# Scores and first mix in an attention kernel as products of 64 rows by 64 columns, in common visits

## The chip, the cores and the metric

The kernel runs on one core of a Trainium2 chip. The metric is device microseconds of one execution; three timed runs of the kernel before have a median of 1301.0 us (1297.99 to 1308.34). The engines are named as in the profile: PE is TensorE (PEld its weight loads), DVE VectorE, ACT ScalarE, POOL GpSimd, SP SyncE.

## The reference

Attention whose heads are mixed before and after the softmax, then two gated feed-forward stages over all tokens. Everything is float32.

```python
# q, k, v: (4, 12, 448, 64); w_pre, w_post: (12, 12)
scores = scale * np.matmul(q, k.transpose(0, 1, 3, 2))
scores = np.einsum('bhij,hg->bgij', scores, w_pre)
scores = scores - np.max(scores, axis=-1, keepdims=True)
attn = np.exp(scores)
attn = attn / (np.sum(attn, axis=-1, keepdims=True) + 1e-09)
attn = np.einsum('bhij,hg->bgij', attn, w_post)
x = np.matmul(attn, v)                     # -> (1792, 768)
x = ((x @ w1) * (x @ w2) @ w3) @ w_out     # first stage, 768 -> 1024 -> 1024 -> 768
h = np.maximum(np.maximum(x @ m1, x @ m2), x @ m3)
return h @ m_out                           # second stage, 768 -> 768 -> 768
```

## The kernel before

**Scores.** A score unit is `scores(b, pr, it)`: 112 queries of one pair of heads. q and k lie with the 64 values of a head on 64 partitions, two heads on 128. So a unit is two products, one on partitions 0 to 63 and one on 64 to 127, each with 112 columns of weights (the queries) and 448 moving columns (the keys), into the two banks of the PSUM tile `s`. Both are plain float32 products; such a product is two matmul rows in the trace. ACT scales and evicts the unit, and it is stored to `sdram` in DRAM, `[query, head, key]`. A batch has 6 x 4 = 24 units, 96 in all.

**First mix and softmax.** `regroup` loads 20 queries back as two blocks of 10, with (query, head) on 120 partitions, one DMA on SP. `mix_softmax` mixes the heads: for each of the two blocks one product with the 120x120 block-diagonal matrix `kp`, into a bank of the tile `m`. The first 62 steps are plain (`plain`): float32, two matmul rows for each product. The other 30 are split: DVE cuts `x` into a high and a low part in `split_scores` (L232, L233), and each product is three fp32r passes (in `products`, L115). DVE then takes the maximum (L250), ACT the exponentials with their sums (L254), and DVE makes `kwr`, the block-diagonal second mixing matrix with the reciprocals of the sums in it (L258 to L261).

**Second mix and v.** `post_mix` (L277) multiplies `e` by `kwr` for the step before, into `p`; ACT evicts it to `a`. After six steps (120 queries) `attend` (L304) multiplies by v, head by head, two heads on the two halves of the columns.

**The dense stages.** Batches 0 and 1 are finished under the attention as fillers: generators that yield after six fp32r passes (w in the rows: `products`, L115). Batches 2 and 3 come after the attention, in `last_two`. Weights arrive as 64-bit words and are cut by ACT and DVE the first time (`from_f64`), later loaded back from DRAM by SP (`slab`, L157 to L159).

**Order.** The main loop has a step for each 20 queries, 23 for a batch, 92 in all. A step calls `regroup` two steps ahead, `split_scores` one step ahead, `mix_softmax`, and then three thirds, in which fillers run at 2.7 or 3.9 yields a step, the units of the next batch are placed (`ahead_scores`), and `post_mix` and `attend` come. What one engine is given stays in program order on it; a tile scheduler moves work by its own priorities before that. The tile `m` exists once (two banks), `s` once, `p` once.

Of the kernel before, what the change touches and what calls it, by code (L numbers as in the profile page):

```python
# [7 lines left out]
F32 = mybir.dt.float32  # L8
# [9 lines left out]
P = 128  # L18
GI = 10
NG = -(-S // GI)  # L20
CG = 12
JC, JP = 4, 112
IT = 4
# [8 lines left out]
PLAIN = 2 * NP + 16  # L32
# [18 lines left out]
def plain(b, p):  # L51

    return b * NP + p < PLAIN
# [3 lines left out]
def attention_talking_heads_moe_kernel(  # L57
# [106 lines left out]
    kp = const.tile([120, GI, H], F32, name="kp")  # L164
    kp_hi = const.tile([120, GI * H], F32R, name="kp_hi")
    kp_lo = const.tile([120, GI * H], F32R, name="kp_lo")
    kw = const.tile([120, H, GI], F32, name="kw")

    def block_diagonals():
        own = const.tile([120, GI], F32, name="own")  # L170
        wide = const.tile([120, 2, H], F32, name="wide")
        nc.gpsimd.dma_start(own, block_mask)
        for x, w in enumerate((w_pre, w_post)):
            nc.gpsimd.dma_start(wide[:, x], bass.AP(w.tensor, w.offset, [[0, GI], [H, H], [1, H]]))
        nc.vector.tensor_mul(
            kp, wide[:, 0].unsqueeze(1).to_broadcast([120, GI, H]), own.unsqueeze(2).to_broadcast([120, GI, H])
        )
        nc.vector.tensor_mul(
            kw, wide[:, 1].unsqueeze(2).to_broadcast([120, H, GI]), own.unsqueeze(1).to_broadcast([120, H, GI])
        )  # L180
        flat = kp.rearrange("p i h -> p (i h)")
        nc.vector.tensor_copy(kp_hi, flat)
        nc.vector.tensor_sub(kp_lo, flat, kp_hi.bitcast(F32))
# [3 lines left out]
    def load_heads():  # L187

        t = [big.tile([P, HP, S], F32, tag=x, name=n) for x, n in (("xhi", "kall"), ("xlo", "qall"))]
        for a, z in ((0, 2), (2, HP)):  # L190
            for dst, src, w in zip(t, (kT, qT), (S, JP)):
                nc.sync.dma_start(dst[:, a:z, :w], src[0, a:z, :, :w].rearrange("x p j -> p x j"))
        nc.sync.dma_start(t[1][:, :, JP:], qT[0, :, :, JP:].rearrange("x p j -> p x j"))
# [8 lines left out]
    def scores(b, pr, it, heads, tag="s", eng=None, out=None):  # L202
        k, q = heads
        st = out if out is not None else pa.tile([JP, 2, S], F32, tag="s", name="s", bufs=2)
        pt = banks(tag)
        for o in range(2):
            sl = slice(o * D, (o + 1) * D)
            nc.tensor.matmul(pt[:JP, o, :S], q[sl, it * JP:(it + 1) * JP], k[sl], start=True, stop=True)  # L208
        if eng is nc.vector:
            nc.vector.tensor_scalar_mul(st, pt[:JP, :, :S], D ** -0.5)  # L210
        else:
            nc.scalar.activation(st, pt[:JP, :, :S], AF.Copy, scale=D ** -0.5)  # L212
        if out is None:
            issue = nc.sync if eng is nc.vector else nc.scalar
            issue.dma_start(sdram[b][it * JP:(it + 1) * JP, 2 * pr:2 * pr + 2], st)

    def regroup(b, p):
        n, m = groups(p)
        r = m * H
        x = pa.tile([120, 2, S], F32 if plain(b, p) else F32R, tag="x", name="x", bufs=AHEAD + 1)  # L220
        src = sdram[b][2 * GI * p:2 * GI * p + n * m].rearrange("(x i) h j -> (i h) x j", x=n)
        nc.sync.dma_start(x[:r, :n] if plain(b, p) else x[:r, :n].bitcast(F32), src)
        xst[b, p] = x

    def split_scores(b, p):
        if plain(b, p):
            return
        n, m = groups(p)
        r = m * H
        x = xst[b, p]  # L230
        xh = pa.tile([120, 2, S], F32R, tag="xh", name="xh", bufs=2)
        nc.vector.tensor_copy(xh[:r, :n], x[:r, :n].bitcast(F32))  # L232
        nc.vector.tensor_sub(x[:r, :n], x[:r, :n].bitcast(F32), xh[:r, :n].bitcast(F32))  # L233
        xst[b, p] = (x, xh)

    def mix_softmax(b, p):
        n, m = groups(p)
        r = m * H
        pt = banks("m")
        x = xst.pop((b, p))  # L240
        for u in range(n):
            if plain(b, p):
# [6 lines left out]
        nmax = pa.tile([120, 2], F32, tag="nmax", name="nmax", bufs=3)  # L249
        nc.vector.tensor_reduce(out=nmax[:r, :n], in_=pt[:r, :n, :S], axis=AX.X, op=ALU.max, negate=True)  # L250
        e = pa.tile([120, 2, S], F32, tag="e", name="e", bufs=LAG + 1)
        den = pa.tile([120, 2], F32, tag="den", name="den", bufs=3)
# [4 lines left out]
        rec = pa.tile([120, 2], F32, tag="rec", name="rec", bufs=3)  # L257
        nc.vector.tensor_scalar_add(den[:r, :n], den[:r, :n], 1e-9)  # L258
        nc.vector.reciprocal(rec[:r, :n], den[:r, :n])
        kwr = pa.tile([120, 2, H * GI], F32, tag="kwr", name="kwr", bufs=LAG + 1)  # L260
# [6 lines left out]
    def post_mix(b, p):  # L267
        n, m = groups(p)
        r = m * H
# [433 lines left out]
    row = pa.tile([JP, H, S], F32, tag="a", name="row", bufs=1)  # L703
    for pr in range(HP):
        scores(0, pr, 0, first[pr], "mps"[pr % 3], nc.vector if pr % 2 else nc.scalar, row[:, 2 * pr:2 * pr + 2])
        if pr % 2:
            sl = slice(2 * pr - 2, 2 * pr + 2)
            nc.sync.dma_start(sdram[0][:JP, sl], row[:, sl])
# [5 lines left out]
    early = [(pr, it) for it in range(1, IT) for pr in range(HP)]  # L714
    heads = {}

    def ahead_scores(b, p, third):

        if b + 1 < B:
# [114 lines left out]
```

## Time and profile before

| | |
|---|---|
| timed runs | 1297.99, 1301.0, 1308.34 us; median 1301.0 |
| profiled execution: span | 1297.0 us, an execution of its own beside the timed ones; median less span 4.0 us |
| mean granted TensorE clock | 0.976 of full speed |
| busy over the span | PE 1229.3 us (95%), PEld 1009.0, DVE 807.5, ACT 611.0, POOL 222.0 |
| first mix: maximum on DVE | 92 times, from 51.3 to 915.7 us |
| score units | 15.3 to 697.6 us |
| HBM | 176.50 MB read, 84.15 MB written |

PE's busy time is modelled at its ends: matmuls are pipelined, and one of 448 columns shows 0.36 us although the next starts 0.205 us later. What a piece of work costs on PE is therefore read from the starts of what stands around it. The span falls into the start (to about 110 us), attention with score units of the next batch and fillers (to about 700), attention of the last batch with fillers (to about 945), and the dense stages of batches 2 and 3.

### The profile page before, as it was taken

The numbers are of one execution on the slowest core, as the hardware profiler recorded it, in microseconds if no ns is written. First come the engines' busy times: TensorE is split into PE (matmuls) and PEld (weight loads), VectorE is DVE, ScalarE is ACT, GpSimd is POOL, SyncE is SP. The second block draws the span as 40 slices with busy tenths as digits, with TensorE's granted clock in tenths as the row PEclk, the third lists the DMA queues.
The fourth block names the chain that finished last, engine by engine and source line by source line (L and its number), as shares of the span: only waits on it lengthen the run. The fifth ranks groups of instructions, "written<-read, shape, count | busy, mean of one in ns | idle before, by whom it ended". The sixth has DMA issues, their size and how long they took to land.

```text
span 1297.0 us, 19342 instructions
## 1 busy us (share of the span) xinstructions
PE 1229.3 (95%) x7438; PEld 1009.0 (78%) x7438; DVE 807.5 (62%) x1251; ACT 611.0 (47%) x1146; POOL 222.0 (17%) x243
## 2 busy tenths in 40 slices
PE   4588999989999999999998999999989999999998
PEld 1246777867777787777777988999978889989887
DVE  5677334448573466867366686965357766368784
ACT  3466555546564455756454444444353334323331
POOL 3343111000000000000456546650000000000000
PEclk6799999999999999999998999999989999999999
DMA  9978768688786569887787987772353332133334
GB/s 288 297 248 255 211 209 293 181 244 265 246 280 200 166 194 289 287 258 243 241 301 235 274 263 238 247 240 88 123 190 98 108 113 68 45 106 104 110 98 133
DMA packets 111987, 261.92 MB, mean 202 GB/s; under 512 B 22868, under 2 KB 66152, under 8 KB 111896
## 3 DMA queue, kind: packets, MB, share of 16 engines
q1 hardware_dynamic: 55736, 116.71, 30.6%
q0 software_dynamic: 15392, 77.62, 18.1%
q10 hardware_dynamic: 40768, 66.37, 15.2%
q8 instruction: 59, 0.97, 0.3%
q14 instruction: 32, 0.26, 0.1%
HBM read 176.50 MB, written 84.15 MB: 201 GB/s over the span
## 4 chain that ended last, share of the span: by engine, by line
PE 77%; DMA 11%; DVE 8%; ACT 3%; issue 2%; POOL 0%; DVEq 0%; ACTq 0%; SPq 0%; POOLq 0%
PE w L115 34%; PE p L277 9%; PE m L115 8%; PE m L243 6%; PE p L115 6%; PE s L115 5%; PE s L304 5%; PE s L208 4%; DMA xdram<-x 2%; DMA xlo<-xdram 2%; DVE wc L104 2%; DMA wlo<-kept_b 1%; DVE nmax L250 1%; DMA sdram<-s 1%; DMA x<-sdram 1%
## 5 line engine op out<-in xcount | busy, mean ns | idle before, releaser
L254 ACT ACTIVATE e<-m,nmax 120x448 f32<-120x448 f32 x180 | 112.6, 631 | 149.3 <-DVE nmax L250 144.5
L277 PEld LDWEIGHTS p<-kwr,e 120*112 120x112 f32 (+1 forms) x1440 | 162.6, 179 | 18.7 <-issue 6.9
L277 PE MATMUL p<-kwr,e 120*112 120x120 f32 (+1 forms) x1440 | 167.9, 270 | 2.5 <-DVE kwr L261 1.3
L250 DVE TENSOR_REDUCE nmax<-m 120x2 f32<-120x896 f32 (+1 forms) x92 | 98.0, 1065 | 106.6 <-PE m L243 84.9
L159 DVE TENSOR_TENSOR wlo<-wlo,whi 128x768 fp32r<-128x768 f32 (+1 forms) x58 | 67.9, 1171 | 100.6 <-ACT whi L158 96.3
L284 ACT COPY a<-p 112x480 f32<-112x480 f32 (+1 forms) x184 | 92.3, 552 | 59.7 <-PE p L277 54.5
L115 PE MATMUL w<-yhi,whi 128*128 128x448 f32 (+1 forms) x292 | 117.6, 403 | 0.0
L115 PE MATMUL w<-hhi,whi 128*128 128x448 f32 (+1 forms) x280 | 112.3, 401 | 4.6 <-ACT hhi L336 4.0
L243 PE MATMUL m<-x,kp 120*120 120x448 f32 (+1 forms) x244 | 106.5, 556 | 6.3 <-DMA x<-sdram 4.4
L115 PE MATMUL w<-hhi,wlo 128*128 128x448 f32 (+1 forms) x280 | 102.6, 367 | 4.3 <-DVE wlo L159 4.3
L115 PE MATMUL w<-yhi,wlo 128*128 128x448 f32 (+1 forms) x292 | 105.4, 361 | 0.0
L115 PE MATMUL w<-ylo,whi 128*128 128x448 f32 (+1 forms) x292 | 105.2, 360 | 0.0
L115 PE MATMUL w<-hlo,whi 128*128 128x448 f32 (+1 forms) x280 | 102.9, 368 | 0.9 <-POOL hlo L337 0.9
L158 ACT CAST whi<-wlo 128x768 fp32r<-128x768 f32 (+1 forms) x58 | 52.2, 900 | 91.3 <-DMA wlo<-kept_w 22.8
L212 ACT ACTIVATE s<-s 112x896 f32<-112x896 f32 x84 | 77.0, 917 | 19.7 <-PE s L208 13.8
L115 PE MATMUL w<-xhi,whi 128*128 128x448 f32 x192 | 80.1, 417 | 3.7 <-ACT xhi L324 3.7
L208 PE MATMUL s<-k,q 64*112 64x448 f32 x288 | 73.5, 588 | 7.6 <-ACT s L212 3.9
L304 PEld LDWEIGHTS s<-a,v 112*64 112x64 f32 x1536 | 73.7, 137 | 6.2 <-issue 3.7
L304 PE MATMUL s<-a,v 112*64 112x120 f32 (+1 forms) x1536 | 77.1, 260 | 0.7 <-ACT s L212 0.5
L101 ACT ACTIVATE wc<-wraw 128x768 f32<-128x768 f32 (+1 forms) x64 | 54.4, 853 | 46.5 <-DMA wraw<-in_w3T 15.1
L243 PEld LDWEIGHTS m<-x,kp 120*120 120x120 f32 (+1 forms) x244 | 43.6, 185 | 39.8 <-issue 26.8
L115 PEld LDWEIGHTS w<-hhi,whi 128*128 128x128 f32 x280 | 53.6, 191 | 25.7 <-issue 13.3
(205 smaller groups left out, 2615.7 us busy)
## 6 DMA issues: line engine op xcount, KB each, us to landing
x<-sdram SPq DMA_DIRECT2D x88, 420.0 KB, 5.0
sdram<-s ACTq DMA_DIRECT2D x84, 392.0 KB, 4.5
wraw<-in_wm POOLq DMA_DIRECT2D x18, 768.0 KB, 6.7
wlo<-kept_m SPq DMA_DIRECT2D x27, 384.0 KB, 3.0
wlo<-kept_w SPq DMA_DIRECT2D x18, 512.0 KB, 4.4
wraw<-in_w3T POOLq DMA_DIRECT2D x16, 512.0 KB, 6.2
kept_m<-wc ACTq DMA_DIRECT2D x18, 384.0 KB, 4.7
wc<-kept_m POOLq DMA_DIRECT2D x18, 384.0 KB, 6.9
```

Source lines behind the costliest of these rows:

```text
L101: nc.scalar.activation(t, high.bitcast(F32), AF.Abs)
L115: nc.tensor.matmul(out, w, r, start=(k == 0), stop=(k == 3 * n_k - 1))
L158: nc.scalar.copy(hi, t)
L159: nc.vector.tensor_sub(lo, t, hi.bitcast(F32))
L208: nc.tensor.matmul(pt[:JP, o, :S], q[sl, it * JP:(it + 1) * JP], k[sl], start=True, stop=True)
L212: nc.scalar.activation(st, pt[:JP, :, :S], AF.Copy, scale=D ** -0.5)
L243: nc.tensor.matmul(pt[:r, u, :S], kp.rearrange("p i h -> p (i h)")[:r, :r], x[:r, u], start=True, stop=True)
L250: nc.vector.tensor_reduce(out=nmax[:r, :n], in_=pt[:r, :n, :S], axis=AX.X, op=ALU.max, negate=True)
L254: nc.scalar.activation(e[:r, u], pt[:r, u, :S], AF.Exp, bias=nmax[:r, u:u + 1], scale=1.0, accum_out=den[:r, u:u + 1])
L277: nc.tensor.matmul(pt[:, jc // 2, jc % 2, :, u * GI:u * GI + m], e[:r, u, jc * JP:(jc + 1) * JP], kwr[:r, u].rearrange("p (g i) -> p g i", ...
L284: nc.scalar.copy(ast[b][:, 2 * x:2 * x + 2, :, off:off + w].rearrange("p c g i -> p (c g) i"), pt[:, x, :, :, :w].rearrange("p c g i -> p ...
L304: nc.tensor.matmul(pt[o * D:(o + 1) * D, pr // 3, pr % 3, :], vst[b][:, jc, h * D:(h + 1) * D], a[:, jc, h, :], start=(jc == 0), stop=(jc ...
```

## The change

A score unit now is four products, each of 64 rows (the values of a head) by 64 columns (64 queries): two heads of a pair and two halves of 128 queries, each on a quarter of TensorE's array. Since 448 is 3 x 128 + 64, the last 64 queries of two pairs make a unit together (a mixed unit, with two stores). A batch has 21 units, 84 in all. The first batch's first row of units is 128 queries wide.

The mix's blocks hold 5 queries: 60 partitions, with zero columns up to 64. A step still has 20 queries, in four blocks: two on partitions 0 to 59 and two on 64 to 123, and each block's product writes 64 partitions of the tile `m`. `kp` is a matrix of 60 rows by 64 columns, twice, one below the other. `regroup` is two DMAs of 60 partitions. All mixes are plain; `plain`, `split_scores`, `kp_hi` and `kp_lo` are gone. Softmax and second mix run on 128 partitions, with zero rows in `kw`.

A unit is issued right ahead of the mix of its step (`some_scores(0)`), others in the thirds. Units for the next batch go into a list (`waiting`) by a new table of steps, and the pair loads have three buffers and are asked for two steps ahead.

```diff
+GB = GI // 2
+HB = 64
+MR = GB * 12
-PLAIN = 2 * NP + 16
...
+def units():
+
+    for pr in range(0, HP, 2):
+        for x in (pr, pr + 1):
+            for it in range(S // P):
+                yield [(x, P * it), (x, P * it + HB)]
+        yield [(pr, S // P * P), (pr + 1, S // P * P)]
...
+            for r in range(2):
+                nc.gpsimd.dma_start(
+                    wide[HB * r:HB * r + MR, x], bass.AP(w.tensor, w.offset, [[0, GB], [H, H], [1, H]])
+                )
...
-        t = [pa.tile([P, S], F32, tag=x, name=x, bufs=2) for x in "kq"]
+        t = [pa.tile([P, S], F32, tag=x, name=x, bufs=3) for x in "kq"]
...
-        for o in range(2):
-            sl = slice(o * D, (o + 1) * D)
-            nc.tensor.matmul(pt[:JP, o, :S], q[sl, it * JP:(it + 1) * JP], k[sl], start=True, stop=True)
+        for c, (pr, i) in enumerate(unit):
+            k, q = heads[pr]
+            for o in range(2):
+                sl = slice(o * D, (o + 1) * D)
+                nc.tensor.matmul(pt[HB * c:HB * c + HB, o, :S], q[sl, i:i + HB], k[sl], start=True, stop=True)
...
+            (pr, i), (other, _) = unit
+            if other == pr:
+                issue.dma_start(sdram[b][i:i + P, 2 * pr:2 * pr + 2], st)
+            else:
+                for c, (pr, i) in enumerate(unit):
+                    issue.dma_start(sdram[b][i:i + HB, 2 * pr:2 * pr + 2], st[HB * c:HB * c + HB])
+
+    def blocks_of(p):
+
+        i = 2 * GI * p
+        return [[(i + GI * r + GB * c, max(0, min(GB, S - i - GI * r - GB * c))) for c in range(2)] for r in range(2)]
 
     def regroup(b, p):
...
+        x = pa.tile([P, 2, S], F32, tag="x", name="x", bufs=AHEAD + 1)
+        for r, row in enumerate(blocks_of(p)):
+            if row[1][1] == GB:
+                src = sdram[b][row[0][0]:row[0][0] + GI].rearrange("(c i) h j -> (i h) c j", c=2)
+                nc.sync.dma_start(x[HB * r:HB * r + MR], src)
+                continue
...
-    def split_scores(b, p):
...
     def mix_softmax(b, p):
...
-        for u in range(n):
-            if plain(b, p):
-                nc.tensor.matmul(
-                    pt[:r, u, :S], kp.rearrange("p i h -> p (i h)")[:r, :r], x[:r, u], start=True, stop=True
-                )
-            else:
-                for _ in products(pt[:r, u, :S], [(kp_hi[:r, :r], kp_lo[:r, :r], x[1][:r, u], x[0][:r, u])], 1):
-                    pass
...
+        for c in range(2):
+            for u, row in enumerate(blocks_of(p)[:n]):
+                sl = slice(HB * u, HB * u + row[c][1] * H)
+                nc.tensor.matmul(pt[HB * c:HB * c + HB, u, :S], kp[sl], x[sl, c], start=True, stop=True)
...
+    def some_scores(third):
         if early:
...
+            scores(0, early.pop(0), first, "s", nc.vector if third == 1 else nc.scalar)
+        elif waiting:
+            scores(*waiting.pop(0))
...
-            if s + 1 < len(steps):
-                split_scores(*steps[s + 1])
+            ahead_scores(*steps[s])
+            some_scores(0)
             mix_softmax(*steps[s])
...
-            if s < len(steps):
-                ahead_scores(*steps[s], third)
+            if third:
+                some_scores(third)
```

On PE, in the second batch's part of the loop, where the next batch's units are made under the first batch's dense stage, the order before has mix (L243) and unit (L208) apart. In these rows w is a filler's PSUM tile, with its row split (xhi, xlo) and weights (whi, wlo), and x2 counts products:

```order
L115 MATMUL w<-xlo,whi 128x448
L115 MATMUL w<-xhi,wlo 128x448
L243 MATMUL m<-x,kp 120x448 x2
L115 MATMUL w<-xhi,whi 128x448
L115 MATMUL w<-xlo,whi 128x448
L115 MATMUL w<-xhi,wlo 128x448
L115 MATMUL w<-xhi,whi 128x448
L115 MATMUL w<-xlo,whi 128x448
L115 MATMUL w<-xhi,wlo 128x448
L208 MATMUL s<-k,q 112x448 x2
L115 MATMUL w<-xhi,whi 128x448
```

On PE at the like place of the changed program (L121 is the line of the dense products, L216 the units, L256 the mix):

```order
L121 MATMUL w<-xhi,whi 128x448
L121 MATMUL w<-xlo,whi 128x448
L121 MATMUL w<-xhi,wlo 128x448
L216 MATMUL s<-k,q 64x448 x4
L256 MATMUL m<-x,kp 64x448 x4
L121 MATMUL w<-xhi,whi 128x448
L121 MATMUL w<-xlo,whi 128x448
```

The unit has moved up to stand right ahead of the mix, and each of them is four products now. From the seventh mix to the 67th there are 50 such common visits, 10 of a unit alone, 10 of a mix alone and one of two units and a mix; before, 21 visits of that stretch join a unit and a mix, 52 are a unit alone and 41 a mix alone (one of these is half a mix). The last 25 mixes stand alone in both.

On DVE, in the last batch, the order before has the split between the weight slab and the sums (L159 makes the low part of a slab, L412 that of a row of y):

```order
L250 TENSOR_REDUCE nmax<-m 120x2
L159 TENSOR_TENSOR wlo<-wlo,whi 128x1024
L232 CAST xh<-x 120x896
L258 TENSOR_SCALAR den<-den 120x2
L233 TENSOR_TENSOR x<-x,xh 120x896
L259 RECIPROCAL rec<-den 120x2
L261 TENSOR_TENSOR kwr<-kw,rec 120x240
```

On DVE in the changed program:

```order
L258 TENSOR_REDUCE nmax<-m 128x2
L165 TENSOR_TENSOR wlo<-wlo,whi 128x1024
L266 TENSOR_SCALAR den<-den 128x2
L267 RECIPROCAL rec<-den 128x2
L269 TENSOR_TENSOR kwr<-kw,rec 128x240
```

The two instructions of the split are gone; the rest stands in the same order.

On SP, late in the loop, before (L222 is `regroup`, L157 a weight slab loaded back):

```order
L222 DMA x<-sdram_78 120x2x448
L157 DMA wlo<-kept_w_1_84 128x1024
L222 DMA x<-sdram_78 120x2x448
L157 DMA wlo<-kept_w_1_84 128x1024
L222 DMA x<-sdram_78 120x2x448
L157 DMA wlo<-kept_m_0_101 128x768
```

On SP in the changed program, close behind that place:

```order
L163 DMA wlo<-kept_m_0_101 128x768
L240 DMA x<-sdram_78 60x2x448 x2
L163 DMA wlo<-kept_m_0_102 128x768
L240 DMA x<-sdram_78 60x2x448 x2
L163 DMA wlo<-kept_m_0_103 128x768
```

Each regroup is two issues instead of one, in the same turn with the slabs.

## Rows read from the trace of the kernel before

**Rows 1.** The page's slices: PE's busy share in tenths, 40 equal slices.
```profile
PE   4588999989999999999998999999989999999998
```

**Rows 2.** Windows: busy us (x instructions) of each engine, PEclk, DMA share, GB/s.
```profile
0.00:110.00 110.00, 71.89 (x278) 36.73 (x278) 74.82 (x105) 52.40 (x96) 40.38 (x50) 0.83 0.89 276
110.00:700.00 590.00, 577.80 (x3808) 447.27 (x3809) 332.59 (x549) 324.99 (x624) 78.44 (x99) 0.99 0.76 241
700.00:945.00 245.00, 237.94 (x1716) 219.15 (x1714) 160.55 (x218) 107.47 (x227) 103.14 (x95) 0.99 0.69 216
```

**Rows 3.** Waits of PE, 110 to 700 us: who <- whom: us, times, longest.
```profile
PE s L208 <- ACT s L212: 3.9, 5, 1.3
PE w L115 <- ACT xhi L324: 3.7, 1, 3.7
```

**Rows 4.** Timeline of PE, 300 to 330 us: start us, us, engine, line.
```profile
303.31 0.37 PE L115 MATMUL w<-xhi,wlo 128*128 128x448 f32 x1
303.52 1.67 PE L243 MATMUL m<-x,kp 120*120 120x448 f32 x4
...
305.23 0.37 PE L115 MATMUL w<-xlo,whi 128*128 128x448 f32 x1
...
306.05 0.36 PE L115 MATMUL w<-xhi,wlo 128*128 128x448 f32 x1
306.33 1.01 PE L208 MATMUL s<-k,q 64*112 64x448 f32 x4
...
307.58 0.36 PE L115 MATMUL w<-xlo,whi 128*128 128x448 f32 x1
```

**Rows 5.** Timeline of PE cut to starts before 306.6 us: that unit.
```profile
306.33 0.63 PE L208 MATMUL s<-k,q 64*112 64x448 f32 x2
```

**Rows 6.** The product with v: starts to 325.9 us, and its line in all.
```profile
325.82 0.32 PE L304 MATMUL s<-a,v 112*64 112x120 f32 x2
...
L304 PE MATMUL s<-a,v x96: 266/266/317, 325.8 to 330.7; 112*64 112x120 f32 x96
```

**Rows 7.** Timeline of PE at a split mix, 821 us.
```profile
820.65 0.36 PE L115 MATMUL m<-x,kp_hi 120*120 120x448 f32 x1
820.86 0.37 PE L115 MATMUL m<-xh,kp_lo 120*120 120x448 f32 x1
```

**Rows 8.** Groups by line: busy us, mean ns, idle before and releasers: the split.
```profile
L233 DVE TENSOR_TENSOR x<-x,xh 120x896 fp32r<-120x896 f32 (+1 forms) x30 | 35.8, 1193 | 0.7
...
L232 DVE CAST xh<-x 120x896 fp32r<-120x896 f32 (+1 forms) x30 | 24.2, 805 | 6.6 <-DMA x<-sdram 6.6
```

**Rows 9.** Tiles m and s: duration ns min/median/max, first and last start.
```profile
L250 DVE TENSOR_REDUCE nmax<-m x92: 609/1083/1093, 51.3 to 915.7; 120x2 f32<-120x896 f32 x88, 96x1 f32<-96x448 f32 x4
...
L212 ACT ACTIVATE s<-s x84: 897/917/942, 29.0 to 698.7; 112x896 f32<-112x896 f32 x84
```

**Rows 10.** The line of regroup: its issues on SP, and to landing.
```profile
L222 SPq DMA_DIRECT2D x<-sdram x92: 317/339/1201, 34.6 to 887.5; - x92
...
DMA to landing us min/median/max: 2.2/4.9/18.2
```

**Rows 11.** Timeline of the start: POOL's load of a mix weight, DVE's first product.
```profile
1.94 0.64 POOL L174 DMA_DIRECT2D wide<-in_w_pre  x1
...
9.47 0.28 DVE L175 TENSOR_TENSOR kp<-wide,own 120x120 f32<-120x120 f32 x1 [8.60 <-DMA wide<-in_w_pre]
```

**Rows 12.** Windows: busy us of each engine, PEclk, DMA share, GB/s.
```profile
25.00:50.00 25.00, 12.50 (x31) 5.49 (x32) 12.59 (x14) 8.90 (x13) 8.34 (x10) 0.64 1.02 344
...
300.00:350.00 50.00, 50.00 (x330) 38.31 (x330) 33.90 (x56) 27.89 (x51) 3.92 (x7) 1.00 0.80 262
350.00:400.00 50.00, 49.93 (x331) 38.57 (x330) 30.47 (x51) 31.28 (x58) 2.86 (x5) 1.00 0.86 282
...
500.00:550.00 50.00, 48.47 (x259) 36.82 (x258) 37.78 (x57) 31.39 (x55) 2.75 (x5) 1.00 0.92 292
...
650.00:700.00 50.00, 45.33 (x304) 37.08 (x303) 31.45 (x40) 23.77 (x49) 29.29 (x29) 0.93 0.80 267
```

More of the change, by code (lines that the diff above doesn't have):

```diff
@@ L236, in mix_softmax @@
     def mix_softmax(b, p):
[L237 to L238 removed]
+        n, _ = groups(p)
+        r = P
         pt = banks("m")
         x = xst.pop((b, p))
[L241 to L248 removed]
@@ L702, in attention_talking_heads_moe_kernel @@
     block_diagonals()
-    row = pa.tile([JP, H, S], F32, tag="a", name="row", bufs=1)
+    row = pa.tile([P, H, S], F32, tag="a", name="row", bufs=1)
     for pr in range(HP):
-        scores(0, pr, 0, first[pr], "mps"[pr % 3], nc.vector if pr % 2 else nc.scalar, row[:, 2 * pr:2 * pr + 2])
+        scores(
+            0, [(pr, 0), (pr, HB)], first, "mps"[pr % 3], nc.vector if pr % 2 else nc.scalar, row[:, 2 * pr:2 * pr + 2]
+        )
         if pr % 2:
             sl = slice(2 * pr - 2, 2 * pr + 2)
-            nc.sync.dma_start(sdram[0][:JP, sl], row[:, sl])
+            nc.sync.dma_start(sdram[0][:P, sl], row[:, sl])
     next(side)
@@ L713, in attention_talking_heads_moe_kernel, with ahead_scores @@
         regroup(*steps[s])
[L714 to L719, printed above, removed]
-            begin = 6 if b == 0 else 2
-            for u in range(HP * IT):
-                at = 3 * begin + u * 3 * (NP - AHEAD - begin) // (HP * IT)
-                if u % IT == 0 and at - 5 == 3 * p + third:
-                    heads[b + 1, u // IT] = load_pair(b + 1, u // IT)
-                if at == 3 * p + third:
-                    scores(b + 1, u // IT, u % IT, heads[b + 1, u // IT])
+    early = sorted((u for u in units() if u[0][1]), key=lambda u: u[0][1])
+    heads, waiting = {}, []
+    def ahead_scores(b, p):
+        if b + 1 == B:
+            return
+        begin, todo = 5 if b == 0 else 2, list(units())
+        steps_of = [begin + x * (NP - AHEAD - begin) // len(todo) for x in range(len(todo))]
+        for x, unit in enumerate(todo):
+            for pr, _ in unit:
+                if pr not in heads and steps_of[x] - 2 == p:
+                    heads[pr] = load_pair(b + 1, pr)
+            if steps_of[x] == p:
+                waiting.append((b + 1, unit, dict(heads)))
+                if unit == todo[-1]:
+                    heads.clear()
+    def some_scores(third):
         if early:
-            pr, it = early.pop(0)
-            scores(0, pr, it, first[pr], "s", nc.vector if third == 1 else nc.scalar)
+            scores(0, early.pop(0), first, "s", nc.vector if third == 1 else nc.scalar)
+        elif waiting:
+            scores(*waiting.pop(0))
     credit = 0.0
@@ L800, in slabs @@
         return c(w.reshape(k // P, P, n // P, P).transpose(2, 1, 0, 3)).reshape(n // P, P, -1).view(np.int64)
+    block_mask = np.zeros((2, HB, GB + GI), np.float32)
+    for r in range(2):
+        for i in range(GB):
+            block_mask[r, H * i:H * i + H, i] = 1.0
+            block_mask[r, H * i:H * i + H, GB + GB * r + i] = 1.0
     return {
```

68 lines of the change are left out of this document (26 added, 42 removed).

## The prediction

> **What bounds the kernel now.** I read the page's slices first, for where TensorE is full; then the windows, cut where the work changes; then what TensorE waits for; then single visits on its timeline.
>
> The slices show TensorE at 9 tenths or more from 130 us on but for four at 8, and from 4 to 8 ahead of that [rows 1]. The windows give the same in numbers: from 110 to 700 us it is busy for 577.8 of 590 us, from 700 to 945 for 237.9 of 245, while DVE has 332.6 and 160.5 there and ACT 325.0 and 107.5 [rows 2]. The granted clock is 0.99 in both, the upper of its two levels. Its waits with a named releaser come to 12.5 us between 110 and 700, in five sums of which the longest are 3.9 and 3.7 us [rows 3]. So in this stretch an amount taken from TensorE's own streams comes off the end, as long as nothing else rises to its place. The first 110 us are different: 71.9 us busy at clock 0.83 with the DMA share at 0.89 [rows 2]. After 945 us nothing is changed.
>
> What a visit costs there is read from starts, since the ends of matmuls are modelled. Four w products start 0.205 us apart (305.23 to 306.05). A first mix of 20 queries, two products, stands between the w at 303.31 and the second w after it at 305.23: 1.92 less two w, 1.51 us for four matmul rows, so 0.378 a pass [rows 4]. A score unit, two products of 64 rows, stands between 306.05 and 307.58: 1.53 less 0.41, 1.12 us [rows 4]. It has four passes as well, but two of them start together at 306.33 [rows 5], so it takes two passes of 0.378 and 0.365 us around them for emptying the array and showing the weight load. Products on two halves of the rows thus run side by side in full. The product with v does the same on two halves of the columns, with different moving data for the two: two start together, and 96 take 325.8 to 330.7, that is 0.102 us a pair for 120 columns [rows 6], where 0.378 for 448 scales to 0.101.
>
> **The change part by part.** The order of the changed program has 92 first mixes and 84 score units, 96 units before. I count from the seventh mix to the 67th, which is nearly the stretch 110 to 700 us. Before, there are 73 units and 61 mixes, 56 plain ones and 5 split. Six fp32r passes of a split mix start 0.2 us apart, 1.23 us [rows 7]. Sum: 73 x 1.12 + 56 x 1.51 + 5 x 1.23 = 172.6 us.
>
> After, there are 50 visits of a unit and a mix together, 10 of a unit, 10 of a mix and one of two units and a mix. The trace before has no visit on four quarters, so it is bounded. The lower end is that all four products run side by side, since rows and columns each do so by themselves [rows 5, 6]: two passes and 0.365, 1.12 us for a unit or a mix, four passes and 0.365, 1.88, for both, 2.63 for three. The upper end is that a pair runs beside nothing else: four passes and 0.365, 1.88 alone, 3.39 for both, 4.90 for three. I take the lower end, because halves of either kind show no loss and a quarter reads its partitions no more often than the column halves of the product with v do. Sum: 50 x 1.88 + 20 x 1.12 + 2.6 = 119.0, a gain of **53.6 us**.
>
> The last 25 mixes have no unit beside them: 1.23 becomes 1.12, **2.8 us**.
>
> DVE loses the split: 24.2 and 35.8 us in 30 pairs [rows 8]. TensorE waits little there, so I count nothing. If the few waits for a mix after 750 us come from this, it is up to 5 us more. The reduction (1083 ns) and the eviction of a unit (917 ns) [rows 9] are as long on 128 partitions as on 112 or 120, if width is what they pay for; three fewer evictions per batch have no cover to lose. ACT's queue has 84 stores as before, since a mixed unit takes two. Counted at nothing.
>
> A regroup becomes two DMAs of 60 partitions, same bytes. One issue takes 0.339 us on SP and one transfer 4.9 us to land [rows 10], and a mix asks for its rows two steps ahead, some 19 us at 92 reductions from 51.3 to 915.7 us [rows 9]. SP carries 92 issues more, 31 us in all, with the weight loads queued behind each; they are asked for two slabs ahead. Zero, as long as that lead holds; without it each regroup would put 0.34 us on the path. The pair loads k and q have a third buffer and wait for less.
>
> At the start POOL issues four loads of the mix weights instead of two, 0.64 us each [rows 11], and the weight slabs behind them come 1.3 us later; DVE's first product waits until 9.47 us for the first [rows 11]. Fewer units stand in the first steps, but DMA is at 0.89 there. I take **1 us** lost, from -3 to +3.
>
> New waits: the other engines do the same work in 9% less time. TensorE's named waits were 12 us in the main stretch; I let them grow by two thirds, **8 us**. The ends are -3 (waits go with the split) and +25.
>
> Sum on the profiled span: 1297.0 - 53.6 - 2.8 + 1 + 8 = 1249.6. The median of the timed runs is 4.0 above that span, so 1253.6, taken as **1254 us**, 3.6% less.
>
> **The rivals.**
>
> *Pairs take turns.* A quarter shares its rows with one other and its columns with another, and no row here shows both sharings at once. If the second pair starts only when the first is through, a unit needs four passes: 50 x 3.39 + 20 x 1.88 + 4.9 = 212.0, 39.4 more than 172.6, and the last 25 mixes 25 x 0.65 = 16.3 more. With 1 us at the start: **1358**, slower. The decision point is near three passes: 148 sets of products (unit or mix) in 96 visits cost 148 x 0.378 x passes + 96 x 0.365, against 203.4 before, equal at 3.0. For it speaks only that a quarter is new; against it both kinds of halves.
>
> *Strict order.* If a product may start only when the one ahead of it has begun its second pass, n products need n + 1 passes: 2.26 alone, 3.77 together, 5.28 for three, in all 66.4 us more in the main stretch and 25.8 more after: **1394**. The row speaks against it: of the four passes of a unit two start at 306.33 and none between that and 306.6 [rows 5], where this order would start one, and then two 0.378 later.
> The Trainium skill, TensorE: Matmul & The Clock Gate, section Part 3: Packing small matmuls, The mechanism, calls matmuls strict FIFO in the order of the program, "no reordering". By that rule, the program having a product's two passes one behind the other, the time would be that of this rival; the trace disagrees with this reading for two products, and no run here shows four.
>
> *Three passes.* The third and fourth product start when the first pair is in its second pass: 1.50 alone, 2.26 together, 3.01 for three, a gain of 26.6 in the main stretch, a loss of 6.8 after it, with the 1 and the 8: **1290**, within 1%.
>
> *DMA takes over.* Its share is 0.92 in 500 to 550 us and 0.86 in 350 to 400 [rows 12]; it moves the same bytes, and 9% less time there would need 1.0 and 0.94. If five of the stretches of 50 us in which it is at 0.8 or more between 110 and 700 keep their length, 250 of 590 us give nothing back: 53.6 x 0.42 = 23 us less gain, **1277**. Against it: 344 GB/s were moved in one stretch at the start, where the stretch at 0.92 has 292 [rows 12].
>
> That the program does not do what the change says is excluded: the order shows units and mixes of four products of 64 rows in 50 common visits.
>
> **How the numbers follow.** All four side by side 0.70 (1254, from 1238 with the waits shrinking to 1290 with 25 us of new ones and each common visit emptying twice); DMA takes over 0.10; three passes 0.08; pairs take turns 0.10; strict order 0.02. The range 1238 to 1295 holds nine tenths of the first three. About 1% is what a measurement of this kernel can tell from no change. Faster by over 1% are the first two, 0.80 less a little for the upper edge and for a gain eaten up: 0.79; within 1% 0.09; slower 0.12.
>
> **What would show it.** In a common visit four matmuls start within some 30 ns, and the next w but one follows 1.88 us plus two w later. From the seventh mix to the 67th some 46 us are missing, and the last 25 mixes take about as long as before. The split's lines are gone from DVE with no change in TensorE's idle time after 750 us. It is wrong if four starts are not together, if the DMA share stays near 1.0 with TensorE idle for weights or for x, or if ACT's evictions of the units, which hold the two banks of s, come late and TensorE waits for them ahead of a common visit, with the mix behind it.

## The result, and the profile after

The changed kernel takes 1256.6 us (median of 4 runs, 1250.8 to 1259.73) where the kernel before took 1303.15 on the same chip (4 runs, 1297.99 to 1308.34): ratio 0.966, 95% interval 0.9585 to 0.9731. The forecast was 1254. Six more runs on another chip gave 1256.39 against 1300.43, 0.966 (0.9627 to 0.9691). The profiled execution has a span of 1258.0 us and a time of its own of 1259.7. Two executions below lie far above their like (1459 us of dve_load, 2420 us of two_regroups), and the ratios leave them out while the medians keep them.

The page's slices of the changed kernel, PE:

```profile
PE   4688999979999999899999899999899999999998
```

Its windows; the columns are those of [rows 2]. The work that stood in 110 to 700 us before ends at about 653 now:

```profile
110.00:650.00 540.00, 520.31 (x4209) 406.71 (x4209) 318.28 (x530) 311.93 (x608) 69.53 (x89) 0.99 0.78 256
650.00:905.00 255.00, 241.00 (x1799) 199.23 (x1797) 116.42 (x179) 112.23 (x239) 101.63 (x106) 0.98 0.71 225
```

TensorE is still the bound (520 of 540 us, 241 of 255), at a granted clock of 0.99 and 0.98 where it was 0.99 in both, but a little less full than in [rows 2]: 96% and 95% where it was 98% and 97%. The DMA share went from 0.76 to 0.78.

A common visit on the timeline of PE of the changed kernel, 334 to 342 us:

```profile
335.98 0.37 PE L121 MATMUL w<-xhi,wlo 128*128 128x448 f32 x1
336.28 0.98 PE L216 MATMUL s<-k,q 64*64 64x448 f32 x8
337.08 0.93 PE L256 MATMUL m<-x,kp 60*64 60x448 f32 x8
337.94 0.47 PE L121 MATMUL w<-xhi,whi 128*128 128x448 f32 x1
338.26 0.36 PE L121 MATMUL w<-xlo,whi 128*128 128x448 f32 x1
```

The same timeline cut to 336.2 to 336.35 us, and to 337.0 to 337.15:

```profile
336.28 0.61 PE L216 MATMUL s<-k,q 64*64 64x448 f32 x4
...
337.08 0.56 PE L256 MATMUL m<-x,kp 60*64 60x448 f32 x4
```

From the last w ahead to the second w behind there are 2.28 us; less two w of 0.205 that is **1.87 us**, where 1.88 was forecast. Of a unit's eight matmul rows four start within 0.07 us, and so do four of the mix's. Read in the same way, with medians over the stretch, 47 common visits take 1.87, a mix alone 1.11 to 1.12 and a unit alone 1.10 (forecast 1.12).

How far the gain went is read from DVE's maxima, the first one behind the sixth mix and so on. The maxima of the seventh, 67th and last mix in the changed kernel (duration ns, first and last start), each asked for in a window of its own:

```profile
L258 DVE TENSOR_REDUCE nmax<-m x1: 1083/1083/1083, 110.7 to 110.7; 128x2 f32<-128x896 f32 x1
...
L258 DVE TENSOR_REDUCE nmax<-m x1: 1091/1091/1091, 652.7 to 652.7; 128x2 f32<-128x896 f32 x1
...
L258 DVE TENSOR_REDUCE nmax<-m x1: 625/625/625, 873.2 to 873.2; 128x1 f32<-128x448 f32 x1
```

The seventh and the 67th before (the last stands in [rows 9]):

```profile
L250 DVE TENSOR_REDUCE nmax<-m x1: 1084/1084/1084, 110.4 to 110.4; 120x2 f32<-120x896 f32 x1
...
L250 DVE TENSOR_REDUCE nmax<-m x1: 1092/1092/1092, 696.0 to 696.0; 120x2 f32<-120x896 f32 x1
```

| us | before | changed | difference | forecast | changed, repeated |
|---|---|---|---|---|---|
| to the 7th mix | 110.4 | 110.7 | +0.3 | +1 | 109.2 |
| 7th to 67th | 585.6 | 542.0 | -43.6 | -53.6 and +8 of waits | 538.7 |
| 67th to 92nd | 219.7 | 220.5 | +0.8 | -2.8 | 224.7 |
| 92nd to the end | 381.3 | 384.8 | +3.5 | 0 | 382.4 |

So the visits give what was forecast, and some 10 us of it are lost again in the main stretch and 3.6 in the last batch. What TensorE waits for in the changed kernel (us, times, longest), 110 to 653 us, behind the first "..." from 653 to 905, and behind the second the like row of the kernel before, 700 to 945:

```profile
PE w L121 <- ACT xhi L332: 5.9, 1, 5.9
PE s L216 <- ACT s L220: 5.0, 6, 2.1
PE m L256 <- ACT e L262: 4.6, 6, 1.5
PE s L312 <- ACT s L220: 2.5, 3, 1.9
PE p L285 <- ACT a L292: 1.5, 1, 1.5
...
PE m L256 <- ACT e L262: 9.2, 5, 5.3
...
PE m L115 <- ACT e L254: 5.2, 2, 2.9
```

The named waits of the main stretch are 19.5 us, where they were 12.5 [rows 3]. Those of the last batch were 5.2 for a mix that waits for ACT's exponentials, and are 9.2 now. All of these rows name ACT, an engine that is busy for 312 of 540 us. The largest of the last batch shows how such a wait comes about. The timeline of all engines of the changed kernel, 703.5 to 708.2 us (brackets: idle before, and what ended it):

```profile
704.04 0.83 ACT L164 CAST whi<-wlo 128x768 fp32r<-128x768 f32 x1 [11.49 <-DMA wlo<-kept_b]
704.78 0.63 ACT L262 ACTIVATE e<-m,nmax 128x448 f32<-128x448 f32 x1
...
706.16 1.77 PE L256 MATMUL m<-x,kp 60*64 60x448 f32 x8 [5.35 <-ACT e L262]
```

ACT does its work in program order, and the cut of a weight slab stands ahead of the exponentials. The slab comes late, ACT stands for 11.49 us, the exponentials behind it hold the tile `m`, which exists once, and TensorE waits 5.35 us for it. The DMAs of that place in the changed kernel, 688 to 705 us (KB each, median us to landing):

```profile
v<-in_v SPq DMA_DIRECT2D x1, 1344.0 KB, 15.2
...
wlo<-kept_b SPq DMA_DIRECT2D x1, 384.0 KB, 12.0
```

The like place before, 729 to 746 us:

```profile
v<-in_v SPq DMA_DIRECT2D x1, 1344.0 KB, 9.9
...
wlo<-kept_b SPq DMA_DIRECT2D x1, 384.0 KB, 7.7
```

The same slab beside the same load of v took 7.7 us to land before and 12.0 now; why, no row here tells.

A wait also costs more than its own length. The windows ahead of 704.4 us and behind it, in the columns of [rows 2]:

```profile
697.60:704.40 6.80, 3.22 (x20) 2.70 (x18) 0.00 (x0) 0.36 (x1) 3.69 (x5) 1.00 1.04 253
704.40:711.20 6.80, 5.04 (x17) 3.29 (x18) 5.20 (x8) 3.93 (x9) 4.06 (x3) 0.50 0.59 208
```

In the second one TensorE, which had stood since 700.8 us, has a granted clock of 0.50, the lower of its two levels (1.2 GHz), and two w products start 0.37 us apart (710.27 and 710.64) where 0.205 is usual. So some 45% of its busy time in such a stretch is lost, an estimate from these starts: 2.3 us here. In the traces read for it, every stretch at 0.50 between the seventh and the last mix begins in a wait of TensorE's or soon behind one; not every wait is followed by one.

### The profile page after: what moved, and what is told of

It is laid out like the page before. It is cut to its first block, busy times and chain, and to the rows that moved or that the text cites. A ratio compares the mean times of both kernels' runs of the same rounds, so it can differ in the third digit from the quotient of the medians.

```text
span 1258.0 us, 20547 instructions
## 1 busy us (share of the span) xinstructions
PE 1179.4 (94%) x8028; PEld 948.1 (75%) x8028; DVE 745.8 (59%) x1190; ACT 600.0 (48%) x1135; POOL 211.9 (17%) x245
## 4 chain that ended last, share of the span: by engine, by line
PE 62%; DMA 14%; DVE 9%; ACT 6%; issue 2%; ACTq 0%; SPq 0%; DVEq 0%
PE w L121 28%; PE p L285 6%; PE p L121 6%; PE s L312 5%; PE s L121 5%; PE m L121 5%; PE m L256 4%; PE s L216 3%; DMA xlo<-xdram 2%; DMA xdram<-x 2%; DMA wlo<-kept_m 2%; DVE nmax L258 2%; DMA k<-in_kT 2%; ACT e L262 1%; DVE wc L110 1%
## 5 line engine op out<-in xcount | busy, mean ns | idle before, releaser
L285 PEld LDWEIGHTS p<-kwr,e 128*112 128x112 f32 x1440 | 163.3, 179 | 12.5 <-issue 3.5
L262 ACT ACTIVATE e<-m,nmax 128x448 f32<-128x448 f32 x180 | 112.6, 630 | 122.8 <-DVE nmax L258 114.0
L285 PE MATMUL p<-kwr,e 128*112 128x120 f32 (+1 forms) x1440 | 166.7, 269 | 2.5 <-ACT a L292 1.5
L258 DVE TENSOR_REDUCE nmax<-m 128x2 f32<-128x896 f32 (+1 forms) x92 | 98.0, 1065 | 61.0 <-PE m L256 60.9
L121 PE MATMUL w<-hhi,whi 128*128 128x448 f32 (+1 forms) x280 | 108.7, 388 | 12.8 <-ACT hhi L344 12.0
L121 PE MATMUL w<-yhi,whi 128*128 128x448 f32 (+1 forms) x292 | 113.7, 390 | 0.0
L256 PE MATMUL m<-x,kp 60*64 60x448 f32 x720 | 96.3, 566 | 16.4 <-ACT e L262 13.8
L121 PE MATMUL w<-hhi,wlo 128*128 128x448 f32 (+1 forms) x280 | 101.9, 365 | 4.4 <-DVE wlo L165 4.4
L121 PE MATMUL w<-yhi,wlo 128*128 128x448 f32 (+1 forms) x292 | 105.8, 362 | 0.0
L121 PE MATMUL w<-ylo,whi 128*128 128x448 f32 (+1 forms) x292 | 105.4, 361 | 0.0
L121 PE MATMUL w<-hlo,whi 128*128 128x448 f32 (+1 forms) x280 | 102.7, 367 | 0.9 <-DVE hlo L413 0.6
L121 PEld LDWEIGHTS w<-hhi,whi 128*128 128x128 f32 x280 | 53.7, 192 | 39.4 <-issue 18.1
L121 PE MATMUL w<-xhi,whi 128*128 128x448 f32 x192 | 76.4, 399 | 5.9 <-ACT xhi L332 5.9
L220 ACT ACTIVATE s<-s 128x896 f32<-128x896 f32 x73 | 67.3, 921 | 25.2 <-PE s L216 13.7
L121 PEld LDWEIGHTS w<-yhi,whi 128*128 128x128 f32 x292 | 55.3, 189 | 31.6 <-issue 24.8
L448 ACT CAST whi<-wlo 128x768 fp32r<-128x768 f32 x40 | 33.4, 835 | 79.5 <-DMA wlo<-sums_m 21.1
```

Of the source, the lines that this page charges most:

```text
L121: nc.tensor.matmul(out, w, r, start=(k == 0), stop=(k == 3 * n_k - 1))
L220: nc.scalar.activation(st, pt[:, :, :S], AF.Copy, scale=D ** -0.5)
L256: nc.tensor.matmul(pt[HB * c:HB * c + HB, u, :S], kp[sl], x[sl, c], start=True, stop=True)
L262: nc.scalar.activation(e[:r, u], pt[:r, u, :S], AF.Exp, bias=nmax[:r, u:u + 1], scale=1.0, accum_out=den[:r, u:u + 1])
L285: nc.tensor.matmul(pt[:, jc // 2, jc % 2, :, u * GI:u * GI + m], e[:r, u, jc * JP:(jc + 1) * JP], kwr[:r, u].rearrange("p (g i) -> p g i", ...
```

## The experiments

Times are medians; stretches and visits are read as in the result. The theory throughout is the prediction's: four products start together, common visits empty the array once instead of twice, and what is lost again are waits.

**changed_again.** The changed kernel beside the three others of its chip.

> The changed kernel once more, beside the three below on one chip, so that differences of under 10 us can be read. Both theories: a ratio of 0.96 to 0.97 to the kernel before, 1250 to 1260 us; from the 67th mix to the 92nd about 220 us.

1256.39 us, ratio 0.9659 (0.9627 to 0.9691). As expected for the time; the last batch's stretch is 224.7 where the first profile had 220.5. Of these 4 us some 3 are the clock (13.7 us of the stretch at 0.50 in place of 6.8) and 1 is waits, so such a stretch scatters by that much from execution to execution. Main stretch 538.7.

**wide_mix.** Units as in the changed kernel, mixes as two plain float32 products of 120 rows by 120 columns, one DMA for a regroup, no mix split:

```diff
-        for c in range(2):
-            for u, row in enumerate(blocks_of(p)[:n]):
-                sl = slice(HB * u, HB * u + row[c][1] * H)
-                nc.tensor.matmul(pt[HB * c:HB * c + HB, u, :S], kp[sl], x[sl, c], start=True, stop=True)
+        for u in range(n):
+            nc.tensor.matmul(
+                pt[:r, u, :S], kp.rearrange("p i h -> p (i h)")[:r, :r], x[:r, u], start=True, stop=True
+            )
```

> The changed kernel with its scores in quarters as they are, but each mix as two plain products of 120 rows by 120 columns (no split anywhere). Theory (products on quarters run side by side, and the gain is the sum of the visits): from the seventh mix to the 67th a mix costs 1.51 us again and a unit 1.12, 161.5 us against 119.0, and the last 25 mixes 0.39 us more each: 42.5 + 9.8 = 52 us more than the changed kernel, less some 7 us of waits that go again: 1302 to 1309 us. Rival (the gain comes from the split that is gone from DVE, or from the new table of units): close to the changed kernel, 1257 to 1270.

1290.12 us, ratio 0.9937 (0.9894 to 0.9981). A common visit takes 2.61 us, a mix alone 1.51. By these prices the visits of the main stretch cost 160.7 us, 11.9 less than before, and the stretch is 12.3 shorter (573.3): what the visits give arrives. The last 25 mixes are 7.3 longer (227.0; 25 x 0.28 is 7.0). The time lies between the two ranges, in neither. The mix in quarters is most of the gain, as the theory had it, but by the medians 33 us are missing without it and not 45 to 52; why not more was not found.

**mix_only.** The units and their places of the kernel before, the mix and its regroup of the changed one (the lines with a minus in the last diff).

> The kernel before with its 96 units of two products (112 columns) in their old places, and only the mix in quarters, unsplit. Theory: 61 mixes go from 1.51 (five from 1.23) to 1.12 and the last 25 from 1.23 to 1.12, 25 us less than before; 22 visits hold a mix and a unit, and if halves and quarters share a visit without emptying the array in between, 8 us more: 1270 to 1278, with waits up to 1283. Rival (the mix in quarters pays only in a common visit with scores in quarters): 1295 or more.

1287.29 us, ratio 0.991 (0.9872 to 0.9948): neither 1270 to 1283 nor 1295. The prices hold, 1.11 us for a mix and 2.05 for a mix beside a unit, and the last 25 mixes are 2.2 shorter. The visits of the main stretch save 25.3 us, but the stretch is only 10.7 shorter (574.9). PE's waits in it, 110 to 687 us:

```profile
PE s L212 <- ACT s L216: 11.7, 6, 3.6
PE w L118 <- ACT xhi L323: 4.5, 1, 4.5
```

A unit waits for ACT's eviction of the tile `s`, 11.7 us where it was 3.9 [rows 3]. All named waits together are 21.2 us, 8.7 more than before; in wide_mix, which lost nothing, they are 12.2. Most of the other 6 of the missing 15 us is the clock. The stretch from the seventh mix to the 67th, before and in mix_only, in the columns of [rows 2]:

```profile
110.40:696.00 585.60, 573.80 (x3790) 444.43 (x3791) 329.47 (x543) 322.00 (x618) 77.75 (x98) 0.99 0.76 240
...
111.30:686.20 574.90, 556.05 (x4017) 412.99 (x4014) 313.21 (x525) 321.41 (x616) 76.03 (x97) 0.98 0.75 243
```

TensorE is at 0.50 for 23.9 us of it, where it was for 10.2, which by the 45% above costs 4.6 us more.

**apart.** The changed kernel with the unit issued behind the first third's fillers instead of right ahead of the mix:

```diff
-            some_scores(0)
             mix_softmax(*steps[s])
...
+            if not third and s < len(steps):
+                some_scores(0)
```

> The changed kernel with the unit that stands ahead of a mix moved behind the first third's fillers: 121 visits from the seventh mix to the 67th against 71. Theory (a visit costs 0.365 us around its passes): 50 x 0.365 = 18 us more, 1274, less up to 6 us if mixes then wait less for their PSUM tile. Rival (the emptying hides under the weight loads of the neighbours, so a common visit brings nothing): within 4 us of the changed kernel.

1278.84 us, ratio 0.9844 (0.9738 to 0.995). Two visits of 1.11 us stand where one of 1.87 stood: 0.35 us each for some 50 of them is 18 us, and the main stretch is 22.2 longer than the changed kernel's (564.2); its named waits are as long, 19.5 us, and 17.1 us at 0.50 in place of 10.2 cost 3.5 more. A stretch of the timeline of PE:

```profile
329.84 0.37 PE L121 MATMUL w<-xhi,wlo 128*128 128x448 f32 x1
330.14 0.98 PE L256 MATMUL m<-x,kp 60*64 60x448 f32 x8
331.05 0.47 PE L121 MATMUL w<-xhi,whi 128*128 128x448 f32 x1
331.36 0.37 PE L121 MATMUL w<-xlo,whi 128*128 128x448 f32 x1
...
332.47 0.98 PE L216 MATMUL s<-k,q 64*64 64x448 f32 x8
```

The theory holds: about half of the whole gain is that the two come in one visit.

**halves.** Units of 128 queries as two products of 64 rows by 128 columns, everything else as changed:

```diff
+        if unit[0][0] == unit[1][0]:
+            pr, i = unit[0]
+            k, q = heads[pr]
+            for o in range(2):
+                sl = slice(o * D, (o + 1) * D)
+                nc.tensor.matmul(pt[:, o, :S], q[sl, i:i + P], k[sl], start=True, stop=True)
```

> The changed kernel with its 128-query units as two products of 64 rows by 128 columns, in the same visits with the mix in quarters (mixed units stay in quarters). Theory one (what empties the array is a change of the size of the tiles, as between a dense product and a unit): 51 common visits cost 0.2 to 0.365 us more, 1267 to 1275. Theory two (rows cut in the same way are enough): a visit stays at 1.88 and the time within 4 us of the changed kernel. In both a unit alone costs 1.12, since it is two passes either way.

1253.07 us, ratio 0.9676 (0.9585 to 0.9767). The time is theory two's, the visit is at the lower end of theory one's: 40 of them take 2.06 us, 0.19 more than four quarters beside four quarters, as the timeline of PE shows:

```profile
334.42 0.37 PE L121 MATMUL w<-xhi,wlo 128*128 128x448 f32 x1
334.72 1.02 PE L217 MATMUL s<-k,q 64*128 64x448 f32 x4
335.67 0.98 PE L262 MATMUL m<-x,kp 60*64 60x448 f32 x8
336.58 0.47 PE L121 MATMUL w<-xhi,whi 128*128 128x448 f32 x1
336.89 0.36 PE L121 MATMUL w<-xlo,whi 128*128 128x448 f32 x1
```

The 40 x 0.19, 7.6 us, are not seen in the time, whose interval is 24 us wide. The main stretch has them: 543.7 is 5.0 longer than in changed_again, while TensorE waits 2.1 us less in it (15.7 in place of 17.8) and is at 0.50 for 6.8 us in both. So quarters are worth some 7 us to the scores as this stretch of one profile each tells, and one visit in place of two is worth more.

**columns_first.** The order of the four products turned, in units and mixes:

```diff
-        for c, (pr, i) in enumerate(unit):
-            k, q = heads[pr]
-            for o in range(2):
+        for o in range(2):
+            for c, (pr, i) in enumerate(unit):
+                k, q = heads[pr]
```

> The changed kernel with the order of the four products turned: the two halves of the columns next to each other, then the other rows. Theory (each quarter goes on its own): a common visit 1.87 us, a mix alone 1.11, the time that of the changed kernel. Rival (two neighbours run together only if they differ in their rows): a third pass or more, 2.25 us for a common visit, some 20 us more in all.

One time, 1244.17 us, beside 1296.83; visits 1.87, 1.11 and 1.11. The visits are the theory's, the time looked like a gain of the order. Again, with six runs:

> The changed kernel with the order of the four products turned in units and mixes. Theory (four products start together, whatever their order): within 4 us of the changed kernel of this call, visits at 1.87, 1.11 and 1.11 us. Rival (its 1244 us of the first look is a gain of the order): 8 to 14 us less than the changed kernel of this call.

1257.69 us, ratio 0.9667 (0.9628 to 0.9707), 1.3 above changed_again. The order is worth nothing, and the 1244 was a low single time (the six reach from 1250.82 to 1265.77).

**two_regroups.** The kernel before with each regroup as two DMAs of half the partitions:

```diff
-        nc.sync.dma_start(x[:r, :n] if plain(b, p) else x[:r, :n].bitcast(F32), src)
+        dst = x[:r, :n] if plain(b, p) else x[:r, :n].bitcast(F32)
+        for y in range(2):
+            sl = slice(y * r // 2, (y + 1) * r // 2)
+            nc.sync.dma_start(dst[sl], src[sl])
```

> The kernel before with each regroup as two DMAs of 60 partitions, nothing else. Theory (the lead of two steps covers 0.34 us more of SP's time for a step): the time of before, within 5 us. Rival (the changed kernel's new waits are paid to the 92 added issues, which hold up the weight loads behind them): 8 to 15 us more than before.

1295.47 us against 1296.83, ratio 0.9977 (0.9946 to 1.0007). The line of its regroup:

```profile
L225 SPq DMA_DIRECT2D x<-sdram x184: 315/410/1716, 36.7 to 890.3; - x184
...
DMA to landing us min/median/max: 1.9/4.2/11.9
```

92 issues more on SP cost nothing: half the bytes land in 4.2 us where the whole took 4.9 [rows 10].

**dve_load.** The changed kernel with the split's two DVE instructions given back to the last 30 steps, on a tile that nothing reads; TensorE's products stay as changed:

```diff
+        xh = pa.tile([P, 2, S], F32R, tag="xh", name="xh", bufs=1)
+        nc.vector.tensor_copy(xh[:MR, :n], x[:MR, :n])
+        nc.vector.tensor_sub(xh[:MR, :n], x[:MR, :n], xh[:MR, :n].bitcast(F32))
```

> The changed kernel with the split's two instructions given back to DVE for the last 30 steps, one step ahead and into a tile that nobody reads: some 55 to 60 us of DVE's time, beginning some 30 us ahead of the 67th mix. Theory (DVE's relief was worth nothing): within 4 us of the changed kernel. Rival (it paid for part of the gain by mixes that wait less): 5 to 12 us more, with longer waits of mixes for the exponentials.

1265.05 us, ratio 0.9747 (0.9693 to 0.9802), the last batch's stretch 227.8. Beside the changed kernel on one chip:

> The changed kernel with the two DVE instructions of the split given back to the last 30 steps, on a tile that nothing reads. Theory (the prediction's term: DVE's relief is worth nothing while TensorE waits little): within 4 us of the changed kernel of this call. Rival (the last batch's waits hang on DVE): 6 to 10 us more, with the stretch from the 67th to the 92nd mix at 225 us or more, as in the first run of it (227.8).

1263.58 us, ratio 0.9725 (0.9683 to 0.9768), 7.2 above changed_again. The means of the six runs each, 1265.1 and 1257.1, differ by 8, with 5 either way from their scatter. The stretch is 228.8 again, 4.1 above changed_again's. The rival holds for the time. A window of dve_load_again, in the columns of [rows 2]:

```profile
650.00:905.00 255.00, 240.44 (x1769) 198.39 (x1767) 160.36 (x220) 107.56 (x230) 112.78 (x106) 0.97 0.69 218
```

The same window of changed_again:

```profile
650.00:905.00 255.00, 239.14 (x1770) 198.32 (x1769) 118.73 (x178) 110.10 (x234) 103.38 (x106) 0.97 0.71 223
```

DVE has 160.4 us of work in 255 in place of 118.7. These windows reach past the last mix, where other waits lie. TensorE's waits cut to the last 25 mixes, dve_load_again from 647.9 to 876.7 us, and behind the "..." changed_again from 648.0 to 872.6:

```profile
PE m L265 <- ACT e L271: 11.2, 7, 2.6
PE s L321 <- ACT a L301: 1.4, 1, 1.4
...
PE m L256 <- ACT e L262: 10.9, 5, 5.2
```

With two more of 0.3 and 0.2 us they are 13.1 in place of 10.9, which is 2.2 of the 4.1 us; the rest of the 8 was not found. In DVE's order the two instructions also stand at the regroup's transfer (12.8 us in six waits), so whether DVE costs by its work or by standing there is not shown.

**less_first.** The changed kernel with fillers of the first 24 steps at 2.4 yields a step, so that the first batch's dense stage lasts until the next x is there:

```diff
-        rate = 2.7 if s < LAG + NP else 3.9
+        rate = 2.4 if s < LAG + NP else 3.9
```

> The changed kernel with the fillers of the first 24 steps at 2.4 yields a step instead of 2.7, so that some ten yields of the first filler are left when the first batch's attention ends. Theory (5.9 us of the time given back are the one wait for the first batch's x at 261 us, which has nothing to run under it): that wait falls to under 1 us and the time by 4 to 6 us, to about 1251. Rival (another wait takes its place, since the loads of x and of weights stay late): within 2 us of the changed kernel.

1272.06 us, ratio 0.9798 (0.9764 to 0.9833): slower, so the theory fell. The 5.9 us ahead of the first dense product go, but 14.9 us ahead of units come, which name ACT's evictions, 5.9 of them at the same place, from 259.6 us. The largest, on the timeline of the kernel, ACT and PE:

```profile
479.40 1.31 ACT L332 CAST xhi<-xlo 128x1344 fp32r<-128x1344 f32 x1 [11.25 <-DMA xlo<-xdram]
...
482.26 0.93 ACT L220 ACTIVATE s<-s 128x896 f32<-128x896 f32 x1
...
483.24 1.77 PE L216 MATMUL s<-k,q 64*64 64x448 f32 x8 [8.34 <-ACT s L220]
```

It is the same chain as at 704 us: the cut of x stands on ACT ahead of an eviction that TensorE needs. In the changed kernel TensorE waits for x itself at the first batch's, ahead of its first dense product, and no unit waits at the second's (487 us); here it waits at both for what is queued behind x. The waits are not all of the loss: dense work left out under the attention runs later, and the stretch behind the last mix is 390.3 us where changed_again has 382.4.

**x_step_later.** The load of x and its dense stage one step later, at the same 2.4 yields:

```diff
-        if b in X or b > APART or attended[b] < S:
+        if b in X or b > APART or attended[b] < S or now[0] <= ended[b]:
...
-                        fillers.append(moe(b))
+                        begun.append((s + 1, b))
```

> The changed kernel with the load of the finished batch's x and the start of its dense stage one step later, and fillers of the first 24 steps at 2.4 yields in place of 2.7, so that the work lasts until the next is there. Theory (the waits that come with the change are ACT's queue standing at a transfer, the load of x above all): the 5.9 us ahead of the first dense product go and the stretch from the seventh to the 67th mix is 4 to 8 us shorter than the changed kernel's of this call; what is moved past the loop gives up to 6 back, so 1246 to 1258 in all. Rival (the waits belong to the tightness and come up elsewhere): the sum of TensorE's named waits in that stretch stays at 17 us or more and the time is within 4 us or longer.

1272.78 us, ratio 0.978 (0.9746 to 0.9815), 16 above changed_again: main stretch 549.7, 11 longer, with 26.3 us of named waits in place of 17.8. The rival holds. The two lines on ACT and PE at that place:

```profile
480.58 1.31 ACT L334 CAST xhi<-xlo 128x1344 fp32r<-128x1344 f32 x1 [11.45 <-DMA xlo<-xdram]
...
485.29 1.77 PE L216 MATMUL s<-k,q 64*64 64x448 f32 x8 [9.79 <-ACT s L220]
```

The cut starts 1.2 us later than in less_first and still stands ahead of the eviction, so the step didn't take it out of the way. A kernel with the cut behind the evictions in ACT's queue was not run. No kernel here is measurably faster than the changed one.

## Why the prediction was right

**The number.** 1256.6 for 1254 is closer than the terms are, and that is luck in part. On the profiled spans the sum gives 47.4 us; 39.0 came, and 42.0 in the repeat. The medians differ by 46.5 and 44.0: the changed kernel's median lies 1.4 us below its profiled span, and in the repeat 1.4 above, where the sum had added 4.0.

**Four side by side, -53.6 us.** Right, and the step on which it stood, the lower end of a visit, was right to 0.02 us: 1.87, 1.12, 1.10 for 1.88, 1.12, 1.12. *Pairs take turns*, *three passes* and *strict order* would have needed 3.39, 2.26 and 3.77 for a common visit. For the last the rows of four starts settle it: four first passes start together, with no second pass between them. The rule of the Trainium skill that the prediction set against itself (TensorE: Matmul & The Clock Gate, section Part 3: Packing small matmuls, The mechanism: matmuls are strict FIFO, "no reordering") gives strict order only if a product's two passes stand one behind the other in the program. No row shows how the program has the passes, so the runs rule out that reading together with the rule, and not the rule by itself.

**Where the gain is from.** The prediction's sum didn't part it. By the ratios, either half alone gives little (wide_mix 8, mix_only 12 us) and both 44: only when a unit and a mix both take two passes and stand in one visit do they share its 0.365 us, and that alone is some 22 us (apart, which keeps 20 without it; its interval reaches from 7 to 34).

**New waits, +8.** Right in the main stretch in its size (named waits +7.0; 10.0 in all, 6.7 in the repeat) and in its releaser, ACT. The late evictions ahead of units that it named as a sign of being wrong are among them, 5.0 us where it was 3.9. Not foreseen was that ACT does not stand by want of time but by order: it waits for a transfer with work behind it that TensorE needs. Less_first and x_step_later show the chain at the load of x, the changed kernel's own rows at a slab.

**The last 25 mixes, -2.8.** The visits are right (1.11 us), the result is not: the stretch is 0.8 longer, 5.0 in the repeat. The term left out waits here, which it put into the main stretch alone; for a mix they rose from 5.2 to 9.2 us. In the repeat waits (10.9) and clock (13.7 us at 0.50, before 6.8) make up the whole: -2.8 + 5.7 + 2.2 is 5.1.

**DVE's split at nothing.** Mis-sized, as far as the work given back tells. In the changed kernel the same DVE work costs 8 us (3 to 13). TensorE of the kernel before waited little, but of the kernel that comes out of the change that was no longer so. Whether the split cost as much before was not measured.

**Regroup as two DMAs at nothing.** Right (two_regroups: -1.4 us, within the scatter).

***DMA takes over.*** Not as forecast: the share of the main stretch rose from 0.76 to 0.78 only. But in places it is part of it: a slab that lands in 12.0 us in place of 7.7 is what ACT waited for at 704.

**What stays open.** With the clock beside the waits the main stretch adds up to within 2 to 4 us. Against the kernel before, in us (visits by their prices; waits from the seventh mix to the 67th; lower clock by the 45% above):

| | stretch | visits | waits | lower clock | left |
|---|---|---|---|---|---|
| changed | -43.6 | -53.6 | +8.0 | -1.0 | +3.0 |
| changed_again | -46.9 | -53.6 | +6.3 | -2.3 | +2.7 |
| mix_only | -10.7 | -25.3 | +7.3 | +4.6 | +2.7 |
| apart | -21.4 | -35.6 | +8.0 | +2.4 | +3.8 |
| wide_mix | -12.3 | -11.9 | +0.8 | +1.0 | -2.2 |

What is left stands in no row. The waits are 15 to 20 us in the traces of all the kernels above that have the mix in quarters and the fillers' rate unchanged, and 11 to 12 in the three that have not (before, two_regroups, wide_mix); why the shorter mix brings them was not taken apart further. The +3.5 us behind the last mix are +1.1 in the repeat, so no cause is sought.

## What to carry to other kernels

Small products should be brought together in one visit to the array, not only made small: quarters for both kinds gave some 20 us, and one visit for the two some 22 more. Price a visit from the starts of what stands around it, in passes plus a fixed amount; the lower of two such bounds was right here for an arrangement that the trace did not hold. When the bound engine gets tighter, look at the queues of the engines beside it for an instruction that waits for a transfer with wanted work behind it. Read the granted clock behind each wait of the bound engine, since a wait can cost more than it lasts.

## What the runs showed of the hardware

Products of 64 rows by 128 columns right ahead of products of 60 rows by 64 columns cost 0.19 us more in a visit than when both are quarters (2.06 against 1.87; units of 112 columns beside such a mix 2.05, in mix_only). Float32 products on four quarters run side by side in full, whatever the order in which they are issued (columns_first, a common visit 1.87 us). Behind a wait of 5.35 us TensorE's granted clock was 0.50 from 704.4 to 711.2 us, and its products started 0.37 us apart in place of 0.205. A load of 1344 KB took 9.9 us to land in one kernel and 15.2 in the other at the like place, and a slab of 384 KB behind it 7.7 and 12.0.
